# Batch 0 of a spectral layer with fp32 first and last products, and weight bands decoded beside its pairs

## The chip, the cores and the metric

The program runs on one core of one Trainium2 chip. The metric is the device time of one execution in microseconds (us). TensorE (PE in the rows, PEld for its weight loads), VectorE (DVE), ScalarE (ACT), GpSimd (POOL) and SyncE (SP, which issues every DMA of this kernel) each work through a queue of their own and wait for each other by semaphores.

## What is computed

For each of 8 batches of 3008 tokens by 256 channels: a real Fourier transform along the tokens, a complex 256x256 product with bias, a soft threshold of 0.01, and the inverse transform. Then a feed-forward layer over all 24064 tokens.

```
X = rfft(x, axis=1)
Yr = Xr @ w_r - Xi @ w_i + b_r ;  Yi = Xr @ w_i + Xi @ w_r + b_i
Y  = sign(Y) * max(|Y| - 0.01, 0)          # real and imaginary part each
y  = irfft(Y, n=3008, axis=1).reshape(24064, 256)
h  = y @ w_in                               # 256 -> 2048
out = (h * clip(h + 3, 0, 6) / 6) @ w_out   # 2048 -> 256
```

`w_in` and `w_out` arrive as float64 and are passed as pairs of 32-bit words, so the kernel turns them into numbers itself.

## The kernel before, in words

Numbers that TensorE multiplies are mostly kept as two float32r tiles, a rounded one (hi) and what is left (lo). `split` (line 127) makes them: a ScalarE cast for hi, and a subtraction on VectorE or GpSimd for lo. `product` (line 132) then runs three matmuls for one product: lo by hi, hi by lo, hi by hi. A few matmuls take plain fp32 operands instead (lines 356 and 476); the trace shows each as two instructions.

The transform of a batch has four steps. `stage1(b)` (line 246) loads the tokens in seven sets of up to ten rows of a 64x47 grid, makes sums and differences of mirrored columns (lines 270, 271), splits them, multiplies by the 47-point table and stores to the DRAM scratch `scr1`. `middle(b)` (line 333) goes over 12 pairs of frequencies: `s2` loads a pair from `scr1` and multiplies by the 64-point table (fp32), `s3` applies the 256x256 weights (24 matmuls of 256 columns for batch 0), the bias and the threshold, and turns the tile by four small DMAs (`zt<-tc`); `s4` splits it; `s5` multiplies by the inverse 64-point table and stores to `scr2`. `segment(b, k)` (line 448) loads ten rows of `scr2` and finishes the inverse (fp32). `prepare(c)` (line 515) makes, for 512 tokens, the seven split operands `yb` of a fast 2x2 block product.

The feed-forward layer is 376 units: 47 chunks `c` of 512 tokens times 8 bands `f` of 256 hidden features. A unit has seven block products (`phase_a` to `phase_d`, 21 matmuls of 256 columns), a gate, and three units later four products into `po` (`down`, 12 matmuls of 512 columns). Unit `(c, f)` needs input band `f` and output band `f` decoded.

`decode` (line 169) turns one band of 128x512 float64 words into floats: seven VectorE instructions and two on ScalarE; `in_band` (line 192) adds two GpSimd products or sums, four GpSimd sums of blocks and three splits, `out_band` (line 214) two GpSimd products. There are 16 bands. Four are decoded during the loop over the pairs of batch 0 (line 610), the others inside the first units (lines 690 to 692), because every band beyond the first ones takes scratch buffers of the running loop.

The order: lines 604 to 615 run `middle(0)` with steps of `stage1(1)` and bands between them, then two segments and `prepare(0)`. From line 665 the units run; `lay` (line 620) deals the steps of later batches into quarter-unit slots, `stage1(1)` into units 1 to 8, `middle(1)` from unit 9 on, and so on. The slots hang on the number of the unit, not on time. The tile framework's scheduler then orders the instructions of each engine by program order and by its own estimate of when each is ready.

Of the kernel before, what the change touches and what calls it, by code (L numbers as in the profile page):

```python
# [9 lines left out]
F32 = mybir.dt.float32  # L10
F32R = mybir.dt.float32r
I32 = mybir.dt.int32
AF = mybir.ActivationFunctionType
# [8 lines left out]
N1, N2 = 64, 47  # L22
# [29 lines left out]
def constants():  # L52
# [34 lines left out]
    for k in (0, N1 // 2):  # L87
# [6 lines left out]
        "g64": f(g64, P, P),  # L94
        "sgn": f(sgn, P, NK),
# [4 lines left out]
def spectral_ffn(ctx: ExitStack, tc: tile.TileContext, x, w_r, w_i, bias, w_in, w_out, f47, f64, g64, sgn, out):  # L100
# [59 lines left out]

    nc.scalar.activation(out=three, in_=three, func=AF.Relu, scale=1.0)
# [7 lines left out]
    def decode(src, cut, tags):  # L169


        st = space([P, 2, 256, 2], I32, "st", tags[0])
        nc.sync.dma_start(out=st.rearrange("p a c w -> p a (c w)"), in_=cut(src, 2))
        low, high = st[:, :, :, 0], st[:, :, :, 1]
        e = space([P, 2, 256], I32, "e", tags[1])
        m, r = twin([P, 2, 256], I32, "m", tags[2])
        mf, rf = twin([P, 2, 256], F32, "f", tags[3])
        v = nc.vector

        v.tensor_scalar(out=e, in0=high, scalar1=20, scalar2=0x7FF, op0=ALU.arith_shift_right, op1=ALU.bitwise_and)  # L180
        v.tensor_scalar(out=e, in0=e, scalar1=896, scalar2=0, op0=ALU.subtract, op1=ALU.max)
        v.tensor_scalar(out=e, in0=e, scalar1=255, scalar2=1 << 23, op0=ALU.min, op1=ALU.mult)
        v.scalar_tensor_tensor(out=e, in0=high, scalar=-(1 << 31), in1=e, op0=ALU.bitwise_and, op1=ALU.bitwise_or)
        base = e.bitcast(F32)
        v.tensor_scalar(out=m, in0=high, scalar1=9, scalar2=0x7FF, op0=ALU.logical_shift_right, op1=ALU.bitwise_and)
        nc.scalar.activation(out=mf, in_=m, func=AF.Copy, bias=1.0, scale=2.0**-11)
        v.tensor_scalar(out=r, in0=high, scalar1=0x1FF, scalar2=22, op0=ALU.bitwise_and, op1=ALU.logical_shift_left)
        v.scalar_tensor_tensor(out=r, in0=low, scalar=10, in1=r, op0=ALU.logical_shift_right, op1=ALU.bitwise_or)
        nc.scalar.activation(out=rf, in_=r, func=AF.Copy, scale=2.0**-42)
        return mf, rf, base  # L190

    def in_band(f, tags):
        def cut(t, words):
            v = t.rearrange("p (h c) -> p h c", h=2)
            return v[:, :, f * 256 * words : (f + 1) * 256 * words]

        mf, rf, base = decode(w_in, cut, tags)
        nc.gpsimd.tensor_tensor(out=mf, in0=mf, in1=rf, op=ALU.add)
        nc.gpsimd.tensor_tensor(out=mf, in0=mf, in1=base, op=ALU.mult)
        s = space([P, 4, P], F32, "s", tags[4])  # L200
        a11, a12, a21, a22 = mf[:, 0, :P], mf[:, 1, :P], mf[:, 0, P:], mf[:, 1, P:]
        for to, a, b, op in (
            (0, a21, a22, ALU.add),
            (1, s[:, 0], a11, ALU.subtract),
            (2, a11, a21, ALU.subtract),
            (3, a12, s[:, 1], ALU.subtract),
        ):
            nc.gpsimd.tensor_tensor(out=s[:, to], in0=a, in1=b, op=op)
        hi, lo = (t[:, f] for t in win_s)
        split(hi[:, :2], lo[:, :2], mf[:, :, :P])  # L210
        split(hi[:, 2], lo[:, 2], a22)
        split(hi[:, 3:], lo[:, 3:], s)

    def out_band(f, tags):
        def cut(t, words):
            n = 512 * words
            return t[:, f * n : (f + 1) * n].rearrange("p (h c) -> p h c", h=2)

        mf, rf, base = decode(w_out, cut, tags)
        for t, part in zip(wout_s, (mf, rf)):  # L220
            nc.gpsimd.tensor_tensor(out=cut(t, 1), in0=part, in1=base, op=ALU.mult)

    EARLY = ("raw", "yb", "T", "qt", "ot")
    LATE = ("xin", "bt", "tc", "z", "pt")
    bands = [(in_band, 0), (in_band, 1)]
    for f in range(nf):
        bands.append((out_band, f))
        if f + 2 < nf:
            bands.append((in_band, f + 2))
    bands = iter(bands)  # L230

    made = [0]

    def decode_next(how):
        make, f = next(bands)
        make(f, how)
        made[0] += 1
# [3 lines left out]
    split(*f47_s)  # L241


    scr1, scr2 = {}, {}

    def stage1(b):
        scr1[b] = dram.tile([2, N1, NK, D], F32, name="scr1")
        sets = SEGS[-1:] + SEGS[:-1]
        xins = {}

        def load(i):
            n1, n = sets[i]
            rows, w = (R47, 2 * D) if n == 2 * J else (n * NK, D)
            tag = ("xin", "gs", None, "gs", None, "raw", "raw")[i] if b == 0 else "xin"
            if tag == "gs":
                xins[i], xins[i + 1] = twin([P, 2, 2 * D], F32, "xin", tag)
            elif tag:
                xins[i] = space([P, 2, 2 * D], F32, "xin", tag)
# [3 lines left out]
            return rows, w  # L262

        shapes = [load(i) for i in range(len(sets))] if b == 0 else [load(0)]
        for i, (n1, n) in enumerate(sets):
            rows, w = shapes[i]
            xin = xins.pop(i)
            plus, minus = xin[:rows, 0, :w], xin[:rows, 1, :w]
            e = space([P, 2 * D], F32, "e", "r" if b == 0 else "e")[:rows, :w]
            (nc.vector if b == 0 else nc.gpsimd).tensor_tensor(out=e, in0=plus, in1=minus, op=ALU.add)  # L270
            (nc.vector if b == 0 and i % 2 else nc.gpsimd).tensor_tensor(out=plus, in0=plus, in1=minus, op=ALU.subtract)
            for c, src in enumerate((e, plus)):
                q = 2 * i + c
                tag = ("xs", "z", "h")[q % 3 if b == 0 else 0]
                xs = [t[:rows, :w] for t in twin([P, 2 * D], F32R, "xs", tag)]
                split(*xs, src, nc.vector if b == 0 and (c == 0 or i % 2 == 0) else nc.gpsimd)
                ps = room(b == 0 and c)
                product(ps[:rows, :w], [([t[:rows, c * R47 : c * R47 + rows] for t in f47_s[:2]], xs)])
                a = space([P, 2 * D], F32, "a", ("a", "h", "h")[q % 3] if b == 0 else "a")[:rows, :w]
                if c and b == 0 and i in (0, 2, 4):  # L280
                    nc.vector.tensor_copy(out=a, in_=ps[:rows, :w])
                else:
                    nc.scalar.copy(out=a, in_=ps[:rows, :w])
                dst = scr1[b][c, n1 : n1 + n].rearrange("(g j) k d -> (j k) g d", g=w // D)
                nc.sync.dma_start(out=dst, in_=a.rearrange("p (g d) -> p g d", d=D))
                if c and b and i + 1 < len(sets):
                    shapes.append(load(i + 1))
                yield
# [6 lines left out]
    def weights():  # L295

        split(*r)
        yield
        split(*w_four[0], k[2])
        yield  # L300
        for i in range(2):
            nc.scalar.mul(out=w_four[1][i], in_=w_four[0][i].bitcast(F32), mul=-1.0)
            yield
        split(*g64_t)
        yield
        st = space([P, 2 * D], F32, "cst", "ot")
        nc.vector.scalar_tensor_tensor(out=st, in0=r[2], scalar=-1.0, in1=k[2], op0=ALU.mult, op1=ALU.subtract)
        nc.vector.tensor_tensor(out=k[2], in0=k[2], in1=r[2], op=ALU.subtract)
        yield
        split(*w_m, st)  # L310
        yield
        split(*k)
        yield

    for i, _ in enumerate(stage1(0)):
        if i == 7:
            r, k = [loaded(w, P, 2 * D, n, "yb") for w, n in ((w_r, "w_r"), (w_i, "w_i"))]
            nc.sync.dma_start(out=bias_s, in_=bias)
            nc.sync.dma_start(out=sgn_s, in_=sgn)
            g64_t = loaded(g64, P, P, "g64", "ot")  # L320
            w_four += [[space([P, 2 * D], F32R, "w", "yb") for _ in range(2)] for _ in range(2)]
            todo = weights()
        if i >= 8:
            next(todo, None)
    run(todo)
    g64_s = g64_t[:2]
    w_s = [r[:2], w_m, k[:2], *w_four]

# [4 lines left out]
    def middle(b):  # L333
# [7 lines left out]
        def tag(g, own, other):  # L341

            return other if b == 0 and g % 2 else own

# [5 lines left out]
        def s2(g):  # L350
            data, f = bt.pop(g)
            ps = room(b == 0)
# [13 lines left out]
            hi, lo = twin([P, 2, 3, P], F32R, "X", tag(g, "X", "gs"))  # L366
            if b:
                xi = space([P, 2, P], F32, "xi")
                nc.scalar.copy(out=xi, in_=pv[:, :, 1])
            split(hi[:, :, :2], lo[:, :, :2], pv)  # L370
            if b:
                nc.vector.tensor_tensor(out=xi, in0=pv[:, :, 0], in1=xi, op=ALU.add)
                split(hi[:, :, 2], lo[:, :, 2], xi)
# [364 lines left out]
```

## Time and profile before

| | us |
|---|---|
| median of 3 runs (lowest, highest) | 2751.63 (2750.67, 2754.11) |
| span of the profiled execution | 2751.1 |
| PE busy | 2604.7 (95%) |
| DVE busy | 1977.7 (72%) |
| ACT busy | 1833.9 (67%) |
| POOL busy | 834.2 (30%) |

The page gives the whole; the stages are read from busy time by window, then from the waits inside a window, then from the rows of single instructions. A busy share of PE includes the wait of a pipelined matmul for the one before it, so the number of matmuls in a window (behind the x) tells more than the share.

### The profile page before, as it was taken

The numbers are of one execution on the slowest core, as the hardware profiler recorded it, in microseconds if no ns is written. First come the engines' busy times: TensorE is split into PE (matmuls) and PEld (weight loads), VectorE is DVE, ScalarE is ACT, GpSimd is POOL, SyncE is SP. The second block draws the span as 40 slices with busy tenths as digits, with TensorE's granted clock in tenths as the row PEclk, the third lists the DMA queues.
The fourth block names the chain that finished last, engine by engine and source line by source line (L and its number), as shares of the span: only waits on it lengthen the run. The fifth ranks groups of instructions, "written<-read, shape, count | busy, mean of one in ns | idle before, by whom it ended". The sixth has DMA issues, their size and how long they took to land.

```text
span 2751.1 us, 44515 instructions
## 1 busy us (share of the span) xinstructions
PE 2604.7 (95%) x16432; PEld 2325.0 (85%) x16432; DVE 1977.7 (72%) x3222; ACT 1833.9 (67%) x3591; POOL 834.2 (30%) x788
## 2 busy tenths in 40 slices
PE   5765799999999999999999999999999999999999
PEld 3643688988888898888898888988898999999997
DVE  7444777777777777777777777777777777766676
ACT  4443576776676776777776767677676766667766
POOL 3254433333233233233322343133222212122210
PEclk8976899999999999999999999999999999999999
DMA  6532343233213222223222222123221211101000
GB/s 176 167 84 72 100 119 101 62 88 89 68 55 84 79 79 65 70 76 81 79 71 64 82 73 86 54 75 92 68 80 46 67 52 57 43 30 31 16 19 16
DMA packets 150817, 200.50 MB, mean 73 GB/s; under 512 B 16975, under 2 KB 104775, under 8 KB 150599
## 3 DMA queue, kind: packets, MB, share of 16 engines
q1 hardware_dynamic: 150599, 197.65, 25.1%
q8 instruction: 129, 2.11, 0.3%
q14 instruction: 89, 0.73, 0.1%
HBM read 97.45 MB, written 74.97 MB: 63 GB/s over the span
## 4 chain that ended last, share of the span: by engine, by line
PE 68%; DVE 12%; ACT 8%; issue 5%; POOL 4%; DMA 2%; SPq 0%; ACTq 0%; DVEq 0%; POOLq 0%
PE po L136 28%; PE pb L136 15%; PE ps_a L136 9%; PE pc L136 8%; PE pd L136 4%; ACT r L575 3%; PE ps_a L476 3%; DVE r L577 2%; DVE gs L130 2%; ACT gs L129 2%; PE ps_a L356 2%; DVE h L540 2%; DMA xin<-in_x 1%; DVE X L130 1%; DVE tc L406 1%
## 5 line engine op out<-in xcount | busy, mean ns | idle before, releaser
L136 PE MATMUL po<-gs,w_out_hi 128*128 128x512 f32 x3008 | 954.3, 398 | 0.9 <-DVE gs L130 0.9
L577 DVE SCALAR_TENSOR_TENSOR r<-r,h 128x1024 f32<-128x1024 f32 x376 | 478.1, 1271 | 388.6 <-ACT r L575 388.6
L136 PEld LDWEIGHTS po<-gs,w_out_hi 128*128 128x128 f32 x3008 | 568.4, 189 | 74.9 <-DVE gs L130 2.6
L136 PE MATMUL po<-gs,w_out_lo 128*128 128x512 f32 x1504 | 610.8, 407 | 6.2 <-ACT gs L129 3.4
L136 PE MATMUL pb<-yb,w_in_hi 128*128 128x256 f32 x3008 | 606.6, 283 | 0.6 <-POOL yb L130 0.6
L130 DVE TENSOR_TENSOR gs<-r,gs 128x1024 fp32r<-128x1024 f32 x376 | 472.8, 1257 | 122.9 <-ACT gs L129 119.7
L575 ACT ACTIVATE r<-h,three 128x1024 f32<-128x1024 f32 x376 | 433.2, 1152 | 186.8 <-DVE h L540 183.6
L136 PEld LDWEIGHTS pb<-yb,w_in_hi 128*128 128x128 f32 x3008 | 468.4, 192 | 50.8 <-POOL yb L130 1.0
L129 ACT CAST gs<-r 128x1024 fp32r<-128x1024 f32 x376 | 395.9, 1053 | 133.3 <-DVE r L577 119.7
L130 POOL TENSOR_TENSOR yb<-T,yb 128x256 fp32r<-128x256 f32 x188 | 206.2, 1108 | 827.9 <-ACT yb L129 827.7
L136 PE MATMUL pb<-yb,w_in_lo 128*128 128x256 f32 x1504 | 430.3, 286 | 10.8 <-ACT u L537 4.2
L540 DVE TENSOR_TENSOR h<-pc,u 128x256 f32<-128x256 f32 x752 | 313.5, 417 | 71.5 <-PE pc L136 63.5
L537 ACT COPY u<-pb 128x256 f32<-128x256 f32 x752 | 277.3, 371 | 105.8 <-PE pb L136 100.1
L136 PEld LDWEIGHTS pb<-yb,w_in_lo 128*128 128x128 f32 x1504 | 287.1, 191 | 70.0 <-ACT u L537 8.1
L136 PE MATMUL pc<-yb,w_in_hi 128*128 128x256 f32 x1504 | 300.9, 281 | 0.5 <-POOL yb L130 0.5
L136 PEld LDWEIGHTS po<-gs,w_out_lo 128*128 128x128 f32 x1504 | 285.2, 190 | 17.1 <-ACT gs L129 4.4
L568 ACT COPY h<-pb 128x256 f32<-128x256 f32 x376 | 140.3, 373 | 149.1 <-PE pb L136 147.6
L136 PE MATMUL pc<-yb,w_in_lo 128*128 128x256 f32 x752 | 218.7, 291 | 22.1 <-DVE h L540 17.9
L136 PEld LDWEIGHTS pc<-yb,w_in_hi 128*128 128x128 f32 x1504 | 233.1, 190 | 1.6 <-POOL yb L130 0.7
L130 POOL TENSOR_TENSOR xs<-xin,xs 120x512 fp32r<-120x512 f32 (+1 forms) x52 | 68.8, 1322 | 354.7 <-ACT xs L129 281.0
L136 PEld LDWEIGHTS pc<-yb,w_in_lo 128*128 128x128 f32 x752 | 143.2, 190 | 38.0 <-DVE h L540 31.7
L540 DVE TENSOR_TENSOR h<-pd,p 128x256 f32<-128x256 f32 x376 | 156.4, 416 | 7.9 <-ACT p L537 6.4
(123 smaller groups left out, 4012.7 us busy)
## 6 DMA issues: line engine op xcount, KB each, us to landing
bt<-scr SPq DMA_DIRECT2D x96, 256.0 KB, 3.0
zt<-tc SPq DMA_DIRECT2D x384, 64.0 KB, 2.0
scr<-pt SPq DMA_DIRECT2D x96, 256.0 KB, 2.0
out<-ot SPq DMA_DIRECT2D x94, 256.0 KB, 2.0
xin<-in_x SPq DMA_DIRECT2D x48, 480.0 KB, 4.7
scr<-a SPq DMA_DIRECT2D x96, 240.0 KB, 2.5
qt<-scr SPq DMA_DIRECT2D x96, 240.0 KB, 3.4
f<-in_f SPq DMA_DIRECT2D x96, 128.0 KB, 2.9
```

The lines of the kernel that those rows point to most:

```text
L129: nc.scalar.copy(out=hi, in_=src)
L130: (on or nc.vector).tensor_tensor(out=lo, in0=src, in1=hi.bitcast(F32), op=ALU.subtract)
L136: nc.tensor.matmul(out=ps, lhsT=a, rhs=b, start=start and n == 0, stop=stop and n == len(todo) - 1, skip_group_check=more,)
L356: nc.tensor.matmul(out=psv[:, dh, :, u, :], lhsT=data[:, u, dh * P : (dh + 1) * P], rhs=f[:, u, :], start=True, stop=True,)
L406: nc.vector.tensor_tensor(out=t, in0=t, in1=c, op=ALU.subtract)
L476: nc.tensor.matmul(out=ps[:, cs * w + g * rows : cs * w + (g + 1) * rows], lhsT=qt[:rows, cs, g, dh * P : (dh + 1) * P], rhs=f47_s[2][:row ...
L537: nc.scalar.copy(out=t, in_=ps)
L540: nc.vector.tensor_tensor(out=hs[i][:, u, half * H : (half + 1) * H], in0=ps, in1=keep.pop((i, n)), op=ALU.add)
L568: nc.scalar.copy(out=hs[i][:, 1, :H], in_=pb)
L575: nc.scalar.activation(out=r, in_=h, func=AF.Relu, bias=three, scale=1.0)
L577: nc.vector.scalar_tensor_tensor(out=r, in0=r, scalar=6.0, in1=h, op0=ALU.min, op1=ALU.mult)
```

## The change

Batch 0 gets functions of its own. `first_stage1` and `first_middle` replace `stage1(0)` and `middle(0)`: the 47-point product and the inverse 64-point product take fp32 operands as they are, without a split, and the inverse product takes the two halves of the partitions as two products of 64 rows (table `g64u`), so the four turning DMAs go. The steps of consecutive pairs are written out in a fixed skewed order (pair `g`, `g-1`, `g-2`).

The decode becomes class `Band`, with ten steps of a few instructions, in place in two buffers of five rotating sets. A pass of the loop over pairs makes one step of three or four bands (`exponent` of band n, `sign` of n-1, `rest` of n-2, `sums` of n-3). There are 14 passes; three more ticks follow after `prepare(0)`.

`in_order` adds, for every instruction traced up to and including `prepare(0)`, an edge to the instruction before it on its engine, the DMA queue included. All 15 steps of `stage1(1)` now lie in units 1 to 8, none in batch 0's loop. The weights that only later batches need (`weights()`) are split after `prepare(0)`. The first two segments load at once, and part of `prepare(0)` moves to VectorE. `w_in` is laid out by bands in DRAM.

```diff
+    def in_order():
+        dep = mybir.DependencyInfo(mybir.DependencyClass.NoSync, mybir.DependencyReason.DATA)
+        last = {}
+        for ins in nc.cur_bb.bb.instructions:
...
+            if ins.engine in last:
+                tc.add_manual_dep(ins, last[ins.engine].name, dep, reason="order")
+            last[ins.engine] = ins
+    class Band:
...
+            nc.sync.dma_start(out=st.rearrange("p c w -> p (c w)"), in_=src[:, f * 1024 : (f + 1) * 1024])
+        def exponent(self):      # VectorE
+            nc.vector.tensor_scalar(out=self.t, in0=self.high, scalar1=0x7FFFFE00, ...)
+        def clamped(self):       # ScalarE
+            nc.scalar.activation(out=self.t, in_=self.t, func=AF.Relu, bias=less, scale=8.0)
+        def sign(self):          # VectorE
+            nc.vector.scalar_tensor_tensor(out=t, in0=high, scalar=-(1 << 31), in1=t, ...)
+            nc.vector.tensor_scalar(out=high, in0=high, scalar1=0x1FF, ...)
+        def middle(self):
+            nc.scalar.activation(out=self.high.bitcast(F32), in_=self.high, func=AF.Copy, scale=2.0**-20)
+        def rest(self):          # VectorE
+            nc.vector.scalar_tensor_tensor(out=self.rf, in0=self.low.bitcast(U32), scalar=2.0**-52, in1=more, ...)
+            nc.vector.tensor_scalar(out=self.high, in0=self.t, scalar1=-(1 << 23), ...)
...
+        def lower(self):
+            if not self.into:
+                nc.gpsimd.tensor_tensor(out=wout_s[1][...], in0=rf, in1=base, op=ALU.mult)
+                return
+            nc.gpsimd.tensor_tensor(out=rf, in0=rf, in1=base, op=ALU.mult)
+            nc.gpsimd.tensor_tensor(out=base, in0=self.top, in1=rf, op=ALU.add)
...          # four GpSimd sums of blocks
+    SETS = (("xin", "xs"), ("tc", "X"), ("z", "zt"), ("T", "e"), ("qt", "yb"))
+    def first_stage1():
...
+            for c, src in enumerate(sides.pop(i)):
+                nc.tensor.matmul(out=ps[:rows, :w], lhsT=f47_s[2][...], rhs=src, start=True, stop=True)
...
+        def s5(g):
+            for ri in range(2):
+                for u in range(2):
+                    at = slice(u * N1, (u + 1) * N1)
+                    nc.tensor.matmul(out=ps[u], lhsT=g64u_s[at, ri * P : (ri + 1) * P], rhs=t[at, ri], ...)
...
+        for g in range(NG + 2):
+            n = g + 1
+            on(s2, g)
+            on(constants, g + 2)
+            on(data, g + 2)
+            on(biased, g - 1)
+            on(taken, g)
+            on(shrunk, g - 1)
+            on(s5, g - 2)
+            stage(n - 1, "sign")
+            stage(n - 1, "middle")
+            on(remainder, g)
+            on(s3, g)
+            on(stored, g - 2)
+            on(signed, g - 1)
+            stage(n - 3, "sums_hi")
+            stage(n - 2, "rest")
+            stage(n, "exponent")
+            stage(n - 2, "upper")
+            stage(n - 2, "lower")
+            stage(n, "clamped")
+            stage(n - 3, "lower_blocks")
+            stage(n - 3, "sums_lo")
+            band()
-    mid, nxt, early = middle(0), stage1(1), 0
-    for i in range(3 * (NK // 2)):
-        next(mid)
-        if i >= 6 and i % 4 == 0 and early < 9:
-            early += 1
-            next(nxt)
-        if i % 9 == 7:
-            decode_next(EARLY)
+    run(prepare(0))
+    in_order()
+    for n in range(NK // 2 + 4, len(todo_bands) + 3):
+        tick(n)
+    weights()
-    lay(nxt, rest + 1, 1, 8)
+    lay(stage1(1), 15, 1, 8)
-        if i < nf:
-            while made[0] < min(2 * nf, 2 * i + 5):
-                decode_next(LATE)
```

In `first_middle`, `s2` is the 64-point product, `taken` a ScalarE copy and `remainder` a VectorE subtraction (the split of its result), `biased` two VectorE instructions, `shrunk` one on VectorE for odd pairs and on GpSimd for even ones, `signed` one on ScalarE, `stored` two ScalarE copies and a DMA.

## Rows read from the trace of the kernel before

**Rows 1.** The page, second part: clock granted to TensorE in 40 slices.
```profile
PEclk8976899999999999999999999999999999999999
```

**Rows 2.** Windows: stretch, us, each engine's busy us (instructions), clock, DMA share, GB/s.
```profile
0.00:43.30 43.30, 20.13 (x42) 10.96 (x43) 28.14 (x42) 20.74 (x40) 14.52 (x17) 0.85 0.83 225
43.30:144.40 101.10, 73.02 (x441) 62.27 (x441) 58.71 (x96) 40.43 (x78) 34.04 (x33) 0.87 0.52 147
144.40:155.05 10.65, 3.78 (x16) 3.54 (x16) 1.43 (x4) 1.19 (x5) 2.52 (x2) 0.59 0.29 82
155.05:300.00 144.95, 88.65 (x340) 69.66 (x341) 76.67 (x146) 61.14 (x122) 72.49 (x75) 0.67 0.24 70
300.00:350.00 50.00, 43.10 (x283) 38.18 (x283) 40.67 (x62) 31.69 (x63) 20.29 (x16) 1.00 0.43 122
...
450.00:500.00 50.00, 50.00 (x321) 44.91 (x320) 35.59 (x58) 36.02 (x72) 13.71 (x14) 1.00 0.26 77
500.00:2751.00 2251.00, 2228.77 (x14361) 2008.17 (x14359) 1658.94 (x2692) 1571.71 (x3070) 635.13 (x596) 1.00 0.22 64
```

**Rows 3.** Waits from 155 to 300 us: who for whom, total us, times, longest.
```profile
POOL f L198 <- ACT f L189: 31.8, 5, 7.2
...
PE pd L136 <- DVE w_in_lo L130: 29.7, 5, 8.8
```

**Rows 4.** Windows of tile xs: the split operands of stage1, same columns.
```profile
43.30:155.00 111.70, 6.83 (x21) 3.41 (x21) 0.00 (x0) 4.13 (x7) 10.16 (x8) 0.84 0.50 141
```

**Rows 5.** DMA from 0 to 45 us: totals; issues by tile, KB each, median us to landing.
```profile
DMA packets 6630, 9.84 MB, mean 219 GB/s; under 512 B 669, under 2 KB 4629, under 8 KB 6629
...
xin<-in_x SPq DMA_DIRECT2D x6, 480.0 KB, 9.1
scr<-a SPq DMA_DIRECT2D x12, 240.0 KB, 2.8
```

**Rows 6.** Chain that ended last, 0 to 300 us: start, us, what.
```profile
87.64 2.88 PE ps_a L136 x24
...
96.69 0.89 PE pb L356 x8
...
146.46 3.09 DMA qt<-scr
149.59 3.80 PE ps_a L476 x16
```

**Rows 7.** Lines by form, 0 to 150 us: count, busy us, mean ns, idle before.
```profile
L394 DVE TENSOR_TENSOR tc<-ps_a,bias 128x512 f32<-128x512 f32 x12 | 8.3, 690 | 31.0 <-PE ps_a L136 31.0
...
L129 ACT CAST X<-pb 128x512 fp32r<-128x512 f32 x12 | 7.0, 581 | 0.9 <-PE pb L356 0.8
L409 ACT ACTIVATE tc<-tc,sgn 128x256 f32<-128x256 f32 x13 | 6.5, 510 | 7.0 <-DVE tc L406 6.8
...
L185 DVE TENSOR_SCALAR m<-st 128x512 int32<-128x512 int32 x5 | 3.7, 742 | 0.0
...
L183 DVE SCALAR_TENSOR_TENSOR e<-st,e 128x512 int32<-128x512 int32 x5 | 3.4, 681 | 0.0
...
L186 ACT ACTIVATE f<-m 128x512 f32<-128x512 int32 x5 | 3.1, 628 | 2.3 <-DVE m L185 2.3
...
L182 DVE TENSOR_SCALAR e<-e 128x512 int32<-128x512 int32 x5 | 2.1, 417 | 0.0
```

**Rows 8.** Lines by form, GpSimd alone, 155 to 300 us, same columns.
```profile
L208 POOL TENSOR_TENSOR s<-f 128x128 f32<-128x128 f32 x10 | 6.4, 663 | 0.4
...
L199 POOL TENSOR_TENSOR f<-f,e 128x512 f32<-128x512 f32 x5 | 6.3, 1263 | 0.4
...
L208 POOL TENSOR_TENSOR s<-s,f 128x128 f32<-128x128 f32 x5 | 2.5, 501 | 0.0
```

**Rows 9.** Timeline about 50 us: start, us, engine, instruction.
```profile
50.45 1.34 POOL L199 TENSOR_TENSOR f<-f,e 128x512 f32<-128x512 f32 x1
50.57 1.51 DVE L185 TENSOR_SCALAR m<-st 128x512 int32<-128x512 int32 x1
```

More of the change, by code (lines that the diff above doesn't have):

```diff
@@ L99, in spectral_ffn @@
 @with_exitstack
-def spectral_ffn(ctx: ExitStack, tc: tile.TileContext, x, w_r, w_i, bias, w_in, w_out, f47, f64, g64, sgn, out):
+def spectral_ffn(ctx: ExitStack, tc: tile.TileContext, x, w_r, w_i, bias, w_in, w_out, f47, f64, g64, g64u, sgn, out):
     nc = tc.nc
@@ L192, in in_band @@
[L192 to L229, printed above, removed]
@@ new lines, in spectral_ffn, with band, stage, tick @@
+    todo_bands = [(into, f) for f in range(nf) for into in (1, 0)]
+    SETS = (("xin", "xs"), ("tc", "X"), ("z", "zt"), ("T", "e"), ("qt", "yb"))
+    bands = []
+    def band():
+        n = len(bands)
+        if n < len(todo_bands):
+            bands.append(Band(*todo_bands[n], SETS[n % len(SETS)]))
+    def stage(n, what):
+        if 0 <= n < len(todo_bands):
+            getattr(bands[n], what)()
+    def tick(n):
+        stage(n - 3, "sums_hi")
[9 more added lines that the diff above has]
+        band()
@@ L248, in stage1, with tag @@
         sets = SEGS[-1:] + SEGS[:-1]
-        xins = {}
+        xins, shapes = {}, {}
+        ahead = 2 if b == 1 else 1
+        def tag(n, own, other):
+            return other if b == 1 and n % 2 else own
         def load(i):
+            if i >= len(sets):
+                return
             n1, n = sets[i]
[L253 to L258, printed above, removed]
+            rows, w = shapes[i] = (R47, 2 * D) if n == 2 * J else (n * NK, D)
+            xins[i] = space([P, 2, 2 * D], F32, "xin", tag(i, "xin", "tc"))
             at = n1 // J * 2 * D
@@ L261, in load @@
             nc.sync.dma_start(out=xins[i][:rows, :, :w], in_=src)
-            return rows, w
-        shapes = [load(i) for i in range(len(sets))] if b == 0 else [load(0)]
+        for i in range(ahead):
+            load(i)
         for i, (n1, n) in enumerate(sets):
@@ L295, in weights @@
     def weights():
[L297 to L303, printed above, removed]
         split(*g64_t)
-        yield
-        st = space([P, 2 * D], F32, "cst", "ot")
+        st = space([P, 2 * D], F32, "cst", "bt")
         nc.vector.scalar_tensor_tensor(out=st, in0=r[2], scalar=-1.0, in1=k[2], op0=ALU.mult, op1=ALU.subtract)
         nc.vector.tensor_tensor(out=k[2], in0=k[2], in1=r[2], op=ALU.subtract)
-        yield
         split(*w_m, st)
-        yield
         split(*k)
[L313 to L326, printed above, removed]
-    w_s = [r[:2], w_m, k[:2], *w_four]
+    first = first_stage1()
+    next(first)
+    r, k = [loaded(w, P, 2 * D, n, "ot") for w, n in ((w_r, "w_r"), (w_i, "w_i"))]
+    w_four += [[space([P, 2 * D], F32R, "w", "yb") for _ in range(2)] for _ in range(2)]
+    w_s = [r[:2], w_m, k[:2], *w_four]
+    mid = first_middle()
+    for i in range(len(SEGS)):
+        next(first)
+        if i == 4:
+            split(*r)
+        if i == 5:
+            split(*w_four[0], k[2])
+    g64u_s = space([P, 2 * P], F32, "g64u", "p1")
+    nc.sync.dma_start(out=bias_s, in_=bias)
+    nc.sync.dma_start(out=sgn_s, in_=sgn)
+    next(mid)
+    band()
+    next(mid)
+    band()
+    nc.sync.dma_start(out=g64u_s, in_=g64u)
+    for n in range(2):
+        nc.scalar.mul(out=w_four[1][n], in_=w_four[0][n].bitcast(F32), mul=-1.0)
+    split(*f47_s)
+    tick(0)
+    run(mid)
+    tick(NK // 2 + 3)
     def part(pair, sl):
@@ L523, in prepare @@
             t = space([P, 2, H], F32R, "yb")
-            split(t[:, 0], t[:, 1], src, nc.gpsimd)
+            split(t[:, 0], t[:, 1], src, some(n in (7, 4)))
             yb[c, n] = (t[:, 0], t[:, 1])
```

322 lines of the change are left out of this document (245 added, 77 removed).

## The prediction

> **What bounds the kernel now.** I read the page first, then busy time by window, then the waits of the worst window, then single prices. The page's clock line is full from the sixth slice on and below it before [rows 1]: the trouble lies in the first 300 us. The windows split that stretch [rows 2]. From 500 us to the end PE is busy 2228.8 of 2251 us at full clock; nothing before it changes what follows, because the later work hangs on unit numbers. The first 43.3 us are near what DMA can do (share 0.83, 225 GB/s) while PE holds only 42 matmul records. From 43.3 to 144.4 the 12 pairs take 101 us, 8.4 each. From 155.05, the first feed-forward matmul, until 300 us there are only 340 matmuls in 145 us, at clock 0.67; until 350 us 283 in 50; from 450 to 500 us 321 in 50, the saturated rate, 0.156 us each. In the poor stretch PE waits for decoded bands: 29.7 us in five waits on the last lo block of an input band, and that chain's GpSimd step waits 31.8 us for the decode's second ScalarE result [rows 3]. So the units run at the decode's pace, not at PE's.
>
> The sum therefore has three terms: T0, when the first unit starts; U, from there to the state that the old kernel has at 350 us; and the rest, 2751.1 - 350 = 2401.1 us, unchanged. Before, T0 = 155.05 and U = 194.95.
>
> **T0, first part: up to the first pair.** The change takes 14 splits (a cast and a subtraction each) out of the first step. PE gets dearer: an fp32 matmul of 128 columns costs 2 x 0.111 us at full clock (0.89 us for 8 instructions, rows 6), so 512 columns cost 0.89 us instead of three float32r matmuls, and 13 full equivalents 11.6 us; at the low clock (3.80 us for 16 of 120 columns, rows 6) twice that plus, some 24 us. Starting at 5 us that ends between 17 and 29 us. But bytes decide: before the first pair can be read, 3.07 MB of x, 3.07 MB of stores, 0.51 MB of w_r and w_i, 0.25 of bias, 0.25 of tables, 0.51 of the first band, 0.25 of data and 0.1 of f47 must pass, 8.0 thousand KB or 8.2 MB (sizes of the x loads and stores in rows 5). At 225 GB/s [rows 2] that is 36.6 us, and with 1.3 us before the first load 38. The old order moved 9.84 MB by 45 us [rows 5], the difference being bands and early x loads. I take 38; the ends are 34 (stores overlap better) and 43 (no gain).
>
> **T0, second part: the pairs.** A pass of the new loop, per engine:
> - PE: s2 0.89 and s3 2.88 [rows 6]. s5 is four fp32 products of 64 rows by 256 columns, a form not in the trace. Nearest is the 128-column row: twice its columns, 0.45 us each, 1.8 us. If halves of the rows ran at once it would be 0.9; at low clock 3.6. I take 1.8, the row's own rate. Sum 5.6 us.
> - DVE: biased 0.69 and a clamp of 0.42, shrunk 0.68 every other pass, remainder 0.68, sign 0.68 + 0.42, rest 0.68 + 0.42, exponent 0.42, sums_lo 0.68 every other pass: 5.1 us by the undisturbed prices [rows 7].
> - ACT: taken 0.58, middle, upper and clamped 0.63 each, signed 0.51, two half copies for stored 0.75, sums_hi and lower_blocks about 0.65 per pass together: 4.4 us [rows 7], the half copies by the 0.58 us of a whole one plus a start.
> - POOL: an input band has two of 1.26 and four sums of 0.45 to 0.66, 4.8 us; an output band 1.26; so 3.0 per pass, plus half a shrunk, 3.7 us [rows 8].
> - DMA: 0.13 + 0.26 + 0.26 + 0.52 MB = 1.18 MB, 5.2 us at 225 GB/s. SP issues four DMAs per pass instead of eight. The band's load stands at the end of the pass, so what waits behind SP's wait for a free buffer is the next pair's table and data, and these have over one pass of slack.
>
> Five engines at 3.7 to 5.6 us in fixed queues don't reach 5.6. The step that ties them is s3 of a pair, then biased, shrunk, sign and remainder on DVE, then the last third of the next s3: 1.1 + 0.7 + 1.1 + 0.7 + 1.0 us and some 0.5 of hand-overs, 5.1 us; it fits, but leaves DVE no room. What DVE meets is GpSimd: a VectorE instruction with a single SBUF input took 1.51 us, not 0.42, beside a GpSimd product [rows 9]; over five of them the mean is 0.74 against 0.42 for one that met none [rows 7]. With four such per pass that is 0 to 1.3 us, so DVE is 5.1 to 6.4. I take 6.2 us per pass; the ends are 5.6 (PE) and 7.4 (below).
>
> So: 38, plus 4 for the first pass with a cold PE, plus 12 x 6.2 = 74, gives 116. The last pair's threshold, sign, s5 and store take about 8 us; store and load of the segments about 6 (3.09 for a load, rows 6): 130. Before, the first unit matmul came 5.5 us after that load [rows 2, 6]. Now both segments stand ahead of it in the fixed order, another 3.2 us: T0 = 139.
>
> **U.** From 155.05 to 350 us PE did 340 + 283 = 623 matmuls. 21 matmuls of stage1(1) that ran before 155 us [rows 4] now come into it, 16 of the second segment leave it: 628 at 0.156 us are 98 us. The cover that hid those 21 (a PE waiting in the pair loop) is gone; they cost 3.3 us in U. Filling the pipe costs about 8 us (no down products for three units, cold clock), and the other engines some 5%: the three last ticks and weights() are queued on DVE, ACT and POOL ahead of the first gate, and in units 1 to 8 stage1(1) puts DVE at about 7 us per unit beside PE's 6.9. U = 98 / 0.95 + 8 = 111; its ends are 102 (98 plus half of the filling loss) and 127 (the 300 to 350 rate, 283/321 = 0.88, and twice the filling loss: 98 / 0.88 + 16).
>
> **Sum.** 139 + 111 + 2401 = 2651 us; that is 16 us from T0 and 84 from U. The median before is 0.5 us over the profiled span, so the median should be 2651 too.
>
> **The rivals.**
> 1. GpSimd and VectorE shut each other out in the pair loop. DVE's SBUF-only work, 3.75 us per pass, and POOL's 3.7 then add up to 7.4 us; 12 passes by 1.2 more: 2665 us, with slower units 2680. For it: rows 9. Against: the PSUM-reading steps run beside GpSimd, and most instructions keep their price. The Trainium skill speaks for it (Advanced Engine Details and Errata, Mode Summary): the second VectorE port to SBUF is shared with GpSimd, so that two-port instructions and GpSimd block one another. By that rule alone the time is this rival's; the trace agrees in the stretched instruction of rows 9, while the mean of rows 7 shows that only part of them is hit.
> 2. The first units stay bound by something other than bands: DVE, ACT and the leftover ticks hold PE to the rate of the 300 to 350 window. U = 127, 2667 us. For it: DVE was busy 40.7 of 50 us there [rows 2].
> 3. PE keeps the low clock in the pair loop. 5.6 us become 11 and the loop 12 x 5 us longer: 2711 us. Against: from 43.3 to 144.4 the clock was 0.87 with far fewer columns [rows 2].
> 4. Slower than before: the fixed order makes a convoy, with each engine standing at the head of its queue for the engine before it. Place: the 14 passes. Price: without any overlap a pass is 5.6 + 5.1 + 4.4 + 3.7 = 18.8 us, 12.6 more than taken, 14 x 12.6 = 176 us, 2827. It decides from a pass of about 14 us, where 14 x 7.8 eats the 100 us. Against: nearly each step reads what an earlier pass made.
> 5. The change doesn't do what it says: the scheduler leaves bands to the units, PE waits on w_in_lo go on, U stays near 195 and only T0 moves: 2735. Little speaks for it, since 16 bands are written out by the third tick after prepare(0).
>
> **How the numbers follow.** Forecast (2634 to 2664) 0.60, rival 1 0.15, rival 2 0.12, rival 3 0.06, rival 4 0.04, rival 5 0.03. The forecast's low end is 5.6 us per pass, 7 us less, and U = 102, 9 us less; below it I leave some room for a quicker start. The range goes from 2626 to 2695, past rivals 1 and 2. Faster or slower is counted from 0.2% (5.5 us), about what a measurement can tell: faster 0.95, same 0.01, slower 0.04.
>
> **What would show it.** The windows: the first s2 near 38 us; passes of 6.2 us between s2 starts; the first pd matmul near 139 us; from there 320 matmuls per 50 us within 20 us; no wait of pd on w_in_lo; the state of 350 us, 628 matmuls after the first pd, near 250 us. DVE single-input instructions beside POOL tell rival 1; the granted clock from 45 to 125 us rival 3. The prediction is wrong if units still start with gaps over 2 us, or if the rest after those takes other than 2401 us.

## The result, and the profile of the changed kernel

The changed kernel takes 2661.5 us (median; 2659.1 to 2662.6) against 2751.2 on the same chip: a ratio of 0.967, with a 95% interval of 0.966 to 0.969. The forecast was 2651, the range 2626 to 2695.

The page of the kernel after: whole span, busy engines, granted clock by slices. The clock line answers to [rows 1].

```profile
span 2659.2 us, 44445 instructions
...
PE 2572.4 (97%) x16478; PEld 2303.3 (87%) x16478; DVE 1968.7 (74%) x3168; ACT 1822.2 (69%) x3598; POOL 806.4 (30%) x764
...
PEclk8889999999999999999999999999999999999999
```

Windows of the kernel after, columns as in [rows 2], which they answer to.

```profile
0.00:31.00 31.00, 15.81 (x29) 5.84 (x30) 10.38 (x19) 9.02 (x16) 8.89 (x11) 0.92 0.94 278
...
45.00:115.00 70.00, 53.37 (x401) 45.54 (x400) 68.70 (x98) 39.26 (x94) 41.87 (x44) 1.00 0.52 163
115.00:143.00 28.00, 11.24 (x43) 8.91 (x43) 18.98 (x33) 13.89 (x34) 14.87 (x17) 0.56 0.40 114
143.00:155.00 12.00, 9.86 (x47) 8.45 (x46) 10.58 (x21) 7.12 (x20) 9.86 (x10) 0.62 0.24 61
155.00:200.00 45.00, 39.91 (x222) 33.59 (x220) 32.38 (x43) 32.97 (x63) 25.06 (x21) 0.96 0.47 125
200.00:250.00 50.00, 47.32 (x317) 43.16 (x317) 40.40 (x64) 33.45 (x70) 15.73 (x16) 1.00 0.42 113
...
500.00:2659.00 2159.00, 2136.00 (x13759) 1924.82 (x13758) 1589.19 (x2578) 1506.20 (x2943) 605.44 (x574) 1.00 0.22 63
```

What to see: in the loop over the pairs (45 to 115 us) VectorE is busy 68.7 of 70 us, and nothing else comes near. From 115 to 143 us no engine is: that is the drain between the last pair and the first unit. From 200 us on PE does its saturated 317 matmuls in 50 us, where [rows 2] had 340 in 145 us.

The timeline of PE, at the starts of `s2` in three passes (L370): 6.4 and 6.7 us apart. The last two lines are the segments' first products and the first feed-forward matmul.

```profile
57.16 0.61 PE L370 MATMUL pb<-f,bt 128*128 128x128 f32 x4
...
63.56 0.61 PE L370 MATMUL pb<-f,bt 128*128 128x128 f32 x4
...
70.25 0.50 PE L370 MATMUL pb<-f,bt 128*128 128x128 f32 x3
...
128.10 3.80 PE L697 MATMUL ps_a<-f_all,qt 120*128 120x120 f32 x16 [8.36 <-DMA qt<-scr]
...
142.08 0.58 PE L138 MATMUL pd<-yb,w_in_lo 128*128 128x256 f32 x1 [0.80 <-ACT yb L131]
```

The waits of the kernel after from 142 to 260 us, longest first, answer to [rows 3]:

```profile
POOL xs L132 <- ACT xs L131: 37.1, 9, 14.0
DVE r L799 <- ACT r L797: 9.4, 10, 2.5
POOL e L507 <- DMA xin<-in_x: 8.7, 3, 4.3
...
PE ps_a L138 <- POOL xs L132: 2.5, 2, 1.7
...
PE po L138 <- DVE gs L132: 2.2, 1, 2.2
```

The two PE lines are the longest waits of PE. No wait of PE for a decoded block is left, where [rows 3] had 29.7 us. By units, the lead over the old kernel is 13 us at the first `pd` matmul (155.1 to 142.1), 28 at unit 3, 88 at unit 7 and 94 at unit 14 (347.7 to 253.5); at the last unit it is 92.

### The profile page after: what moved, and what is told of

Its sections match the earlier page's. It is cut to its first block, busy times and chain, and to the rows that moved or that the text cites. A ratio compares the mean times of both kernels' runs of the same rounds, so it can differ in the third digit from the quotient of the medians.

```text
span 2659.2 us, 44445 instructions
## 1 busy us (share of the span) xinstructions
PE 2572.4 (97%) x16478; PEld 2303.3 (87%) x16478; DVE 1968.7 (74%) x3168; ACT 1822.2 (69%) x3598; POOL 806.4 (30%) x764
## 4 chain that ended last, share of the span: by engine, by line
PE 70%; DVE 11%; ACT 8%; issue 3%; POOL 2%; DMA 2%; SPq 0%; ACTq 0%; DVEq 0%; POOLq 0%
PE po L138 30%; PE pb L138 15%; PE ps_a L138 9%; PE pc L138 8%; PE pd L138 4%; ACT r L797 3%; DVE r L799 3%; PE ps_a L697 2%; DVE gs L132 2%; ACT gs L131 2%; PE ps_a L586 2%; DVE h L762 2%; DMA xin<-in_x 1%; DVE X L132 1%; DVE tc L627 1%
## 5 line engine op out<-in xcount | busy, mean ns | idle before, releaser
L132 DVE TENSOR_TENSOR gs<-r,gs 128x1024 fp32r<-128x1024 f32 x376 | 473.3, 1259 | 120.4 <-ACT gs L131 117.0
L132 POOL TENSOR_TENSOR yb<-T,yb 128x256 fp32r<-128x256 f32 x186 | 205.5, 1115 | 834.0 <-ACT yb L131 833.9
L132 POOL TENSOR_TENSOR xs<-xin,xs 120x512 fp32r<-120x512 f32 (+1 forms) x49 | 65.3, 1333 | 346.1 <-ACT xs L131 277.1
```

What stands on the lines that cost most here:

```text
L132: (on or nc.vector).tensor_tensor(out=lo, in0=src, in1=hi.bitcast(F32), op=ALU.subtract)
```

## The experiments

All times are medians beside the kernel before on the same chip, which took 2750 to 2752. A unit's start is that of its first `pd` matmul in the timeline.

### What bounds a pass over the pairs

**Block sums left out.** In `lower`, the GpSimd sum and the four block sums of an input band go; the decoded input bands are then not those of the reference.

```diff
             nc.gpsimd.tensor_tensor(out=rf, in0=rf, in1=base, op=ALU.mult)
-            nc.gpsimd.tensor_tensor(out=base, in0=self.top, in1=rf, op=ALU.add)
...
-                nc.gpsimd.tensor_tensor(out=s[:, to], in0=p, in1=q, op=op)
...
```

> Leaves out, for every input band, the GpSimd sum of upper and lower part and the four block sums (the decoded input bands are not the reference's); the GpSimd work of an input band falls from about 5.5 to 1.2 us, VectorE's instructions stay the same. Theory A (a pass is bound by VectorE, whose instructions GpSimd stretches): passes shrink from 6.55 to 5.3 to 5.9 us and the first unit starts 8 to 14 us earlier, total 2645 to 2652 us. Theory B (a pass is bound by its chain through the fixed queues): passes 6.4 to 6.6 us, total 2657 us or more.

Measured: 2646.3 us. Passes alternate between 5.0 and 6.5 us, the first unit starts at 127.4, 14.7 us earlier, and 15.8 us are kept from unit 1 on. Only GpSimd's work was taken away, and VectorE's pass became shorter, as theory A said. Its window:

```profile
45.00:115.00 70.00, 53.95 (x409) 46.03 (x408) 65.07 (x112) 46.50 (x113) 20.06 (x17) 0.94 0.56 178
```

**The same sums on VectorE.** The five instructions become a step `summed` on VectorE, one pass later.

```diff
+        def summed(self):     # on nc.vector: the sum and the four block sums
...
+            stage(n - 3, "summed")
             on(biased, g - 1)
```

> The in-band's sum of the two parts and its four block sums move from GpSimd to VectorE (a step of their own one pass later); the amount of work is unchanged. Theory A, the VectorE that bounds the pass is slow because GpSimd works beside it: the 5 instructions cost VectorE about 0.68 + 4 x 0.2 = 1.5 us per input band, 0.75 per pass, but without GpSimd's share its work took 65.1 / 12.2 passes = 5.35 us in the kernel that leaves these sums out, whose passes were 5.76; so VectorE comes to 6.1 us and the pass to 6.1 to 6.3 instead of 6.55; the first pd matmul comes 3 to 6 us earlier, and the total is 2 to 6 us lower. Theory B, VectorE's amount of work bounds the pass and GpSimd is only the place of some of it: the pass grows by 0.75 us to 7.3, the first pd by 9 us, the total by about 9.

Measured: 2663.3 us, the first unit at 144.5 (+2.4), +2.2 at unit 14. Passes alternate between about 8 and 6 us, mean 7.1 where the changed kernel has 6.55. Theory B has the pass nearly right (7.3) and the sign, but not the total: of the 6.8 us by which the last `s3` is later (116.8), the drain gives back 4.4. A's price for the move was too low. Its VectorE lines by form, 45 to 115 us (count, busy us, mean ns, idle before), then the same operations in the changed kernel:

```profile
L206 DVE SCALAR_TENSOR_TENSOR t<-st,t 128x512 int32<-128x512 int32 x10 | 6.8, 683 | 0.0
...
L417 DVE TENSOR_SCALAR tc<-tc 128x512 f32<-128x512 f32 x10 | 4.3, 426 | 0.3
L422 DVE TENSOR_TENSOR tc<-tc 128x512 f32<-128x512 f32 x6 | 4.1, 690 | 0.2
...
L243 DVE TENSOR_TENSOR st<-t,st 128x512 f32<-128x512 f32 x5 | 3.5, 693 | 4.6 <-POOL st L237 4.6
L253 DVE TENSOR_TENSOR t<-st 128x128 f32<-128x128 f32 x10 | 2.9, 289 | 0.5
```

```profile
L416 DVE TENSOR_TENSOR tc<-tc 128x512 f32<-128x512 f32 x7 | 10.0, 1424 | 0.2
...
L206 DVE SCALAR_TENSOR_TENSOR t<-st,t 128x512 int32<-128x512 int32 x10 | 8.4, 844 | 0.0
...
L411 DVE TENSOR_SCALAR tc<-tc 128x512 f32<-128x512 f32 x11 | 6.3, 576 | 0.3
```

The stretch was there and it went: the subtraction `shrunk` falls from 1424 to 690 ns, the clamp from 576 to 426. But per input band the five sums take VectorE 0.69 + 4 x 0.29 = 1.85 us, and it waits 0.9 for GpSimd's product ahead of them: 1.4 us per pass. What GpSimd's sums had cost it by the stretch is less: 68.7 us over 10.7 passes, less 65.1 us over 12.2 passes in the kernel without block sums, is 1.1 us per pass.

**The subtraction on PE.** `shrunk` goes from VectorE and GpSimd; `s5` multiplies the value and the clamped value separately, the latter by a negated table, and PSUM adds.

```diff
-                        lhsT=g64u_s[at, ri * P : (ri + 1) * P],
-                        rhs=t[at, ri],
...
+                for n, table in enumerate((g64u_s, g64n_s)):
+                    for u in range(2):
...
+                            lhsT=table[at, ri * P : (ri + 1) * P],
+                            rhs=t[at, n, ri],
...
-            on(shrunk, g - 1)
```

> The subtraction of the clamped value (shrunk) leaves VectorE and GpSimd: s5 multiplies the value and the clamped value separately, the latter by a negated table, and TensorE adds both in PSUM; ScalarE signs both in one instruction. In the loop this takes 7 VectorE instructions of 1.42 us and the GpSimd ones between them away from 10 passes, about 1.0 us of VectorE per pass, and adds four fp32 products of 64 rows to TensorE, 0.85 us per pass, where TensorE was busy 53.4 of 70 us. Theory A, work that really leaves VectorE shortens the pass and is kept, as when the block sums were left out: passes of 5.5 to 5.9 us, the first pd 8 to 12 us earlier (130 to 134), of which most is kept, total 2650 to 2655. Theory B, a change that only moves work to another engine comes to nothing by unit 8, as with the sums on VectorE and with 8 or 12 bands in the loop: the total stays at 2659 to 2664.

Measured: 2654.9 us (2653.0 to 2656.2), ratio 0.9653 (0.964 to 0.9667). Passes take 5.9 us, the first unit starts at 134.4 (7.6 earlier), and 7.1 us are kept at unit 14, 6.2 at the last: theory A. Apart from the kernel without block sums it is the quickest here. Its interval and the changed kernel's overlap slightly, though the two traces differ by 4.8 us in span. Its window:

```profile
45.00:100.00 55.00, 55.00 (x451) 49.31 (x449) 51.22 (x80) 37.74 (x86) 28.99 (x34) 1.00 0.56 182
```

PE is now busy all of 55 us, VectorE 51.2: the bound has gone over to PE. The kernel with the old decode, further down, has five passes of 5.01 us in which PE is never idle either, with four products in `s5` instead of eight:

```profile
73.60:98.60 25.00, 25.00 (x201) 22.49 (x200) 14.96 (x28) 10.35 (x24) 2.57 (x2) 1.00 0.34 114
```

So the four products more cost 5.89 - 5.01 = 0.88 us of a pass that PE bounds.

**Halves of the rows apart.** In `s5` the loop over the row halves goes outside, so that the two products of one half stand next to each other in PE's queue.

```diff
-            for ri in range(2):
-                for u in range(2):
+            for u in range(2):
+                for ri in range(2):
```

> In s5 of batch 0 the two products of one half of the rows run one after the other, then those of the other half, so that neighbours no longer use different rows of the array. Theory A (two products of 64 rows ran at the same time and a pass is bound by VectorE): s5 takes about 1.7 instead of 0.85 us, passes stay at 6.5 to 6.7 us, total within 3 us of the changed kernel. Theory B (a pass is bound by PE): passes 7.3 us, total 2670 us. Theory C (the overlap is an artefact of the records): s5 as before, nothing moves.

Measured: 2662.3 us, passes still 6.55. But the edit did not pull the two halves apart in time. The timeline of one `s5` in this kernel (an fp32 product is two instructions):

```profile
72.32 0.48 PE L431 MATMUL pd<-tc,g64u 64*128 64x256 f32 x1
72.34 0.48 PE L431 MATMUL po<-tc,g64u 64*128 64x256 f32 x1
72.64 0.38 PE L431 MATMUL pd<-tc,g64u 64*128 64x256 f32 x1
72.66 0.38 PE L431 MATMUL po<-tc,g64u 64*128 64x256 f32 x1
...
73.08 0.38 PE L431 MATMUL pd<-tc,g64u 64*128 64x256 f32 x1
73.09 0.38 PE L431 MATMUL po<-tc,g64u 64*128 64x256 f32 x1
```

`po`'s first instruction, four places behind `pd`'s first in the queue, starts 0.02 us after it. An `s5` has the length it has in the changed kernel, so this run doesn't tell what a longer `s5` would cost. It is also what theory C foretold, that the overlap is an artefact of the records, and this run can't rule that out. The two windows above do, by the length of a pass: one after the other, four such products would cost 1.8 us by the rate of [rows 6], and they cost 0.88.

### What the number of bands in the loop is worth

Three kernels decode only the first bands in the loop and leave the others, step by step in two buffer sets, to the first units.

```diff
+    cap, done = [2], [0]          # [8], [12] in the other two
...
+        if i < nf:
+            ticks(2 * i + max(5, done[0] + 1))
```

> Only 2 of the 16 bands are decoded beside the pairs of batch 0; the other 14 come in the first units, two ticks per unit, in two buffer sets that stage1(1) does not use. Theory A (the gain lies in bands that are ready when the units start): passes fall from 6.55 to 4.8 to 5.5 us, the first unit starts near 125 us, then the units wait for bands again and PE's first 628 matmuls after T0 take 150 to 190 us instead of 114; total 2685 to 2725 us. Theory B (the gain comes from the shorter pair chain, the fp32 products and the order): total 2650 to 2670 us.

> 8 of the 16 bands beside the pairs, 8 in the first units, two ticks per unit, in two buffer sets. Theory A (VectorE is full in the loop, 98%, and has a fifth to spare in the units, 40 of 50 us): the first unit 6 to 10 us earlier and most of that kept, total 2650 to 2658 us. Theory B (what is decoded among the units delays them, as the ticks behind the order did, some 1.5 us per band): total 2666 to 2680 us.

> 12 of the 16 bands beside the pairs, 4 in the first units. Theory A: first unit at 136 to 139 us, total 2655 to 2659 us. Theory B: total 2662 to 2668 us.

A fourth has four bands in the loop, and leaves 12 to the units with the old decode, in one set of buffers that `stage1(1)` does not use.

```diff
+    late_bands += todo_bands[4:]
+    todo_bands = todo_bands[:4]
...
+        if i < nf:
+            while len(late_bands) > max(0, 11 - 2 * i):
+                decode_next()         # the old in_band, out_band
```

> Four bands are decoded beside the pairs as in the kernel before; the other 12 by the old decode (nine steps in one go, one set of scratch buffers, two bands per unit), inside the first units. Theory A, the old decode in the units, one band after the other, is what held the units of the kernel before: the first pd comes near 130 us, units 1 to 8 wait for decoded bands again, and the total is 2715 to 2740, some 55 to 80 us above the changed kernel. Theory B, it is no matter which decode is used, only how many bands are left for the units: as with the 14 stepwise bands in the units (2686) and with two fewer, 2675 to 2690.

Measured (us):

| kernel | bands left to the units | first `pd` | `pd` of unit 14 | between | median |
|---|---|---|---|---|---|
| before | 12, old decode | 155.1 | 347.7 | 192.6 | 2751 |
| old decode | 12, old decode | 119.9 | 286.5 | 166.6 | 2698.0 |
| 2 in the loop | 14, steps | 128.5 | 276.9 | 148.4 | 2686.0 |
| 8 in the loop | 8, steps | 131.5 | 255.8 | 124.3 | 2662.8 |
| 12 in the loop | 4, steps | 136.9 | 255.7 | 118.8 | 2663.0 |
| after | none | 142.1 | 253.5 | 111.4 | 2661.5 |

A band left to the units lets the first unit start sooner and makes the units longer. Down to 8 bands in the loop the two are equal within 2.3 us at unit 14, and within 1.5 in the medians; at 2 the units lose 37 us and the loop gives back 13.6. With 2 bands that is theory A, with 12 theory B by the total, and with 8 the total lies between the two. With the old decode, waits for decoded blocks come back, but not to the 2715 to 2740 of theory A, nor is it as cheap as theory B said. Its waits from 128 to 260 us:

```profile
DVE w_in_lo L132 <- ACT w_in_hi L131: 20.1, 10, 2.9
ACT w_in_hi L131 <- POOL m L293: 18.2, 5, 4.3
PEld pd L138 <- DVE w_in_lo L132: 14.4, 4, 6.8
POOL m L292 <- ACT m L283: 13.0, 4, 4.7
PE pd L138 <- DVE w_in_lo L132: 12.3, 4, 6.4
```

So the 81 us that U fell by (192.6 to 111.4) come apart as follows. 166.6 to 111.4, 55 us, is the decode of 12 bands. If 12 stepwise bands in the units lie between those of 8 and 14, near 140 (an interpolation, not a run), about half of it is the number of bands and half the form of the decode. The other 26 us, 192.6 to 166.6, separate the kernel before from one with as many old bands in the units. Which of the remaining differences they belong to (scratch buffers shared with `stage1(1)`, the steps of `stage1(1)` that ran beside the pairs, the order of the bands) was not tried.

### What the fixed order is worth

```diff
     run(prepare(0))
-    in_order()
```

> The changed kernel without the edges of in_order; nothing else differs. Theory A (the written order is part of the gain): the scheduler mixes later work (weights, last ticks, stage1(1), first units) into batch 0's loop, VectorE is already 98% busy there (68.7 of 70 us from 45 to 115 us), so the loop and T0 get 5 to 25 us longer, the total 2664 to 2685 us. Theory B (the gain is where the bands lie, and the order is worth nothing): within 4 us of the changed kernel, 2656 to 2665 us.

Measured: 2663.3 us. The last `s3` ends at 126.0 instead of 110.0, the first unit starts 4.0 us later, and at unit 14 the difference is 0.2 us: theory B for the total, though the loop did get longer, as theory A said. The windows from the last `s3` to the first unit, without the order and then with it:

```profile
126.00:146.00 20.00, 9.54 (x47) 7.95 (x48) 7.40 (x17) 5.37 (x14) 2.36 (x3) 0.66 0.50 131
```

```profile
110.00:142.00 32.00, 11.39 (x49) 8.76 (x48) 23.72 (x38) 15.02 (x38) 19.27 (x21) 0.63 0.41 119
```

Without the order VectorE has by then made the `sign` and the `rest` of all 16 bands, with it 12 and 11 of them; the others run in the drain, 23.7 us of VectorE instead of 7.4. The order only chooses where the last bands are paid for, in the loop or behind it.

In the other direction, the fixed part is made longer and takes in the last ticks and `weights()`:

```diff
-    in_order()
     for n in range(NK // 2 + 4, len(todo_bands) + 3):
         tick(n)
...
     weights()
+    in_order()
```

> The call of in_order moved behind the three last ticks and weights(), so these stand behind prepare(0) in every queue instead of floating up into the last passes and in front of the segments. Theory A (the drain of 32 us from the last s3 to the first unit, 110 to 142 us, holds some 6 us of floated work on VectorE): first pd matmul at 134 to 138 us, total 2653 to 2657 us. Theory B (the drain is a chain that these instructions only fill): first pd at 141 to 143 us, and the same work now comes later, total 2659 to 2666 us.

Measured: 2669.4 us. The first unit starts 5.0 us earlier, as nothing floats in front of the last pair any more, but unit 5 starts 7.8 us later and unit 14 9.9. Before the first unit VectorE then does none of `weights()` and fewer band steps; the floating work had filled holes of the drain, and in the units it costs twice what the drain gives back. Neither theory had that: A had the start right, and the total is beyond B's.

### What the fp32 products of the first step are worth

```diff
-                nc.tensor.matmul(
...
+                xs = [v[:rows, :w] for v in twin([P, 2 * D], F32R, "xs", ("xs", "z")[c])]
+                split(*xs, src, (nc.vector, nc.gpsimd)[c])
+                product(ps[:rows, :w], [([v[:rows, c * R47 : c * R47 + rows] for v in f47_s[:2]], xs)])
```

> The first step of batch 0 multiplies split operands again (three float32r products after a cast and a subtraction, VectorE for sums, GpSimd for differences), all else as in the changed kernel. Theory A (the first step is bound by bytes, the fp32 products only have to keep up): the last stores go out 2 to 6 us later, the first s2 at 33 to 37 us instead of 31, total 2661 to 2668 us. Theory B (the stores have slack): first s2 at 31 to 32 us, total within 3 us of the changed kernel. Theory C (the whole gain of the first step, 12 us against the kernel before, is the fp32 products): first s2 at 41 to 43 us, total 2670 us or more.

Measured: 2682.1 us. The first `s2` is at 52.9, later than in the kernel before (43.3), and the 22 us stay to the end. PE waits there 12.6 us for VectorE's part of the splits. We read it so that in the fixed order each set waits for the one pair of split buffers; that was not tried by itself. The same kernel was then run without the fixed order:

> The first step with split operands and three float32r matmuls, as in the earlier run, but without the edges that fix the instruction order. It separates the splits from the order they were put in. Theory A, the splits themselves cost the time: the first s2 stays beyond 48 us (52.9 with the order, 30.9 with fp32 operands and the order), and the total is 18 to 24 us above the changed kernel. Theory B, the written order made a convoy of them, with one pair of split buffers: the scheduler lets sums and splits run ahead, the first s2 is at 36 to 43 us (43.3 in the kernel before), and the total is 6 to 12 us above the changed kernel without the order (2663).

Measured: 2675.1 us, the first `s2` at 43.7. The windows of the first 31 us, with the order and without:

```profile
0.00:31.00 31.00, 14.34 (x29) 7.29 (x30) 9.24 (x18) 10.71 (x20) 14.53 (x15) 1.00 0.66 176
```

```profile
0.00:31.00 31.00, 18.25 (x35) 9.23 (x36) 17.79 (x23) 13.24 (x25) 17.23 (x17) 1.00 0.74 192
```

DMA's share falls from the changed kernel's 0.94 to 0.66 and 0.74: the loads and stores wait for the splits. Between the two unordered kernels the splits make the first `s2` 10.9 us later (43.7 against 32.8) and the total 12 us higher, as theory B said. The other 11 of the 22 us came with the order, which was written for other operands.

## Why the prediction was right, and where its terms were off

The change in U was forecast as 84 us and came out as 81, for the reason that the prediction gave in the main: the units no longer wait for bands. The first unit came at 142.1 instead of 139, and that nearness is luck: it hides two errors of 7 and 10 us that go against each other. Against the changed kernel's own span of 2659.2 us the sum was 8.1 us short. By its terms:

| term | predicted | measured | difference |
|---|---|---|---|
| first `s2` | 38 | 30.9 | -7.1 |
| 12 passes and the cold first one | 78 | 78.6 | +0.6 |
| from the loop's end to the first `pd` | 23 | 32.6 | +9.6 |
| U | 111 | 113.7 | +2.7 |
| rest | 2401.1 | 2403.4 | +2.3 |

(The loop's end is the last `s2`, at 102.9, plus one pass of 6.55. U ends at 255.8, where the old kernel's 350 us is reached: 350 less 94.2.)

**First `s2`.** The bytes were right, 8.2 MB against 8.62 until 31 us, of which some is for the second pair. The rate was the failed step: 225 GB/s was the mean of the old start, and that start had waited for splits, as the runs above show. The GB/s line of the first 31 us, in 40 slices, shows what the queue does without them:

```profile
GB/s 0 0 123 258 190 301 238 238 230 235 243 246 241 227 238 238 233 227 243 219 198 259 359 360 358 359 358 361 359 358 361 361 362 380 360 366 355 381 325 367
```

The first store was issued at 6.70 us. Its line among the DMA issues (KB, us from issue to landing):

```profile
scr<-a SPq DMA_DIRECT2D x1, 96.0 KB, 12.1
```

While the loads of `x` run, until 17 us, the rate is about 238; from then on, when the stores run, it is 360. The stores did not run beside these loads: the first one landed at 18.8 us, behind all of them. Whether a start that sends the stores in between would be quicker was not tried. Nor was PE cold: the granted clock of these 31 us was 0.92.

**The passes.** 6.2 was forecast and 6.55 measured (`s2` starts 6.4 and 6.7 us apart in turn; nine passes, from the third pair's `s2` at 44.0 to the last, take 58.8). VectorE bounds them, as the prediction said it might, and by the mechanism it named. It counted only single-input instructions as hit; the rows show that those with two SBUF inputs are hit at least as hard (`shrunk` 1424 ns, and 690 with the sums gone from GpSimd). Rival 1 had the mechanism and too high a price: a pass took 6.55 us, not 7.4. (That 68.7 us of VectorE and 41.9 of GpSimd fit into 70 doesn't settle whether a stretched instruction ran slowly or stood: both count as busy.) The sentence of the Trainium skill that it rested on (Advanced Engine Details and Errata, Mode Summary) names two-port instructions; this trace shows two-input subtractions stretched too.

**`s5` on PE** was mis-sized: 1.8 us taken, 0.85 measured, the lower of the two ends, because the two halves of the rows ran at once; the passes of 5.89 and 5.01 us above bear that out. It changed nothing here, since PE was not the bound; it is what let the version with the subtraction on PE gain.

**The drain** is the largest miss. The prediction gave 8 us to the last pair's tail, 6 to the store and load of the segments, and 8.7 to the segments and `prepare(0)`. Measured from 109.5: the last `s5` ends at 119.7, the segments' products start at 128.1, the first `pd` at 142.1, so 10.2, 8.4 and 14.0. VectorE's timeline shows the first of them:

```profile
110.53 0.68 DVE L410 TENSOR_TENSOR tc<-ps_a,bias 128x512 f32<-128x512 f32 x1
111.13 0.93 DVE L132 TENSOR_TENSOR w_m_lo<-cst,w_m_hi 128x512 fp32r<-128x512 f32 x1
111.98 1.50 DVE L411 TENSOR_SCALAR tc<-tc 128x512 f32<-128x512 f32 x1
113.41 0.99 DVE L132 TENSOR_TENSOR w_i_lo<-cst,w_i_hi 128x512 fp32r<-128x512 f32 x1
```

Splits of `weights()` (L132), which come later in the program and carry no order edge, stand between the steps of the last pair, and so do the steps of the last four bands: the failed step is that the prediction queued both ahead of the first gate, and counted them in U. From the last `s3` to the first unit the drain is 32 us here; 26 with the order drawn later, where nothing floats (110.7 to 137.1); 20 without the order, where the bands are done before (126.0 to 146.1); and 21 with the old decode, with 13.2 us of VectorE in it instead of 23.7 (98.8 to 119.9). GpSimd's share counts too: without the block sums it is 25.5, with 7.2 us of GpSimd instead of 19.3 and nearly as much of VectorE (20.0). The segments' 14.0 have a second part in the clock of 0.56, at which their products take the 3.80 us of [rows 6] again.

**U** was right for partly the wrong reason. 98 us of saturated matmuls and 16 us of loss make it up, where 13 of loss were forecast: 8 to fill the pipe, which no run prices by itself, and 5% for other engines. But the loss lay otherwise: from 143 to 200 us PE did 47 and 222 matmuls in 57 us, 42 us' worth, and then 317 in 50. All of it lies at the start, waits of 1.7 and 2.2 us for GpSimd and VectorE among it, so the saturated rate was reached some 60 us after the first `pd`, not 20. The waits on `w_in_lo` went, as forecast. Of the prediction's own signs of being wrong two showed by a hair: PE stood once for 2.2 us (not for a band), and the rest took 2403.4 us, not 2401. Rivals 2 and 5 are out by U itself (113.7, not 127 or 195), rival 3 by the granted clock of 1.00 from 45 to 115 us, and rival 4 by the passes.

**Where the 84 us of U came from** the prediction told too simply: "the units run at the decode's pace". That pace was set by the number of bands left over, by the form of the decode and by something else, in roughly equal parts by the interpolation above, as the runs with fewer bands in the loop show.

## What to carry to other kernels

Price a prologue by the end of the stages that follow it: six edits that only moved band steps between the loop, the drain and the units changed the first unit's start by 4 to 22 us, and eight units on all of that was gone or turned round; what lasted, for better, took work off the engine that bound the loop or, for worse, kept its first pair waiting. Beside a busy GpSimd, count a VectorE subtraction of two SBUF tiles at twice its price (1424 against 690 ns here), and look for an engine with room that can take the step whole, as PE's accumulation did here. An order fixed by hand holds only as far as it reaches: work traced behind it floats into its last waits.

## What the hardware did that was not expected

Two fp32 products of 64 rows each, on the two halves of the partitions, ran at the same time, a pair in the time of one: four products of 256 columns in 0.85 us by the records, and 0.88 us by the length of a pass that PE bounds. In the records they did so even when the two halves stood four instructions apart in PE's queue, with starts 0.02 us apart. The Trainium skill says that tiles operate independently (TensorEngine Tiling (Array Packing), Key Properties), and the trace agrees.

GpSimd is slowed as well. Of the four 128x128 sums of a band, three took 770 to 788 ns in the mean in the loop of the changed kernel, the last 459:

```profile
L248 POOL TENSOR_TENSOR t<-st 128x128 f32<-128x128 f32 x12 | 9.2, 770 | 0.5
...
L248 POOL TENSOR_TENSOR t<-t,st 128x128 f32<-128x128 f32 x6 | 4.7, 788 | 0.5
L248 POOL TENSOR_TENSOR t<-st,t 128x128 f32<-128x128 f32 x5 | 2.3, 459 | 0.0
```

The last one starts beside `remainder`, which reads PSUM, the others beside VectorE steps that read SBUF alone. That this makes the difference is a reading of the timeline and was not tried.
